# A new list of visits, one kept pair stored earlier, and a re-planned order in a fused attention and expert kernel

## The chip, the cores and the metric

The kernel runs on one core of a Trainium2 chip. The metric is device time in microseconds (us), the median of three runs. Five engines run their own instruction streams in order: PE (TensorE, matmuls; PEld is its weight load), ACT (ScalarE), DVE (VectorE), POOL (GpSimd, idle here but for 0.7 us) and SP (SyncE, which issues every DMA). Streams meet only at semaphores, so an instruction that waits holds up everything behind it on its engine.

## The reference

```python
# x (8, 8, 512, 64), state (8, 8, 32, 64); w_a, w_b (512, 1536), w_out (1536, 512)
scores  = x @ state^T / 8;   a  = softmax over the 32 states;   xread = a  @ state
scores2 = state @ x^T / 8;   a2 = softmax over the 512 tokens;  sread = a2 @ x
t = concat(xread, sread) as (8 * 544 tokens, 512)
out = ((t @ w_a) * (t @ w_b)) @ w_out
```

## The kernel before

**Work.** Everything is done in pairs of reduced-precision parts: a value is split into a high part (`_h`) and the rest (`_l`), and each product is three matmuls (high by high, high by low, low by high). For a batch of 512 tokens `xread` is never formed. Its attention matrix `a` is kept transposed in `at_h`, `at_l` (128 x 2 x 512), and the first layer multiplies it with `state @ w_a` and `state @ w_b`, the "pieces" `p_h`, `p_l`. The 1536 hidden columns are cut in 6 chunks of 256. One batch with one chunk is a *chunk-visit*: 24 wide matmuls `ab<-at,p` and 24 `acc<-wo,g`, 48 in all. The sums over chunks of one visit stay in PSUM (`acc`).

**Chunks.** For chunks 0 and 1 and batches 0 to 3, pieces are made directly (`direct`, L1077) from the batch's states and whole weights. For all else a chunk is "stacked" (L1323): its weights are loaded into `raw`, split into `wq`, and projected (`ms<-wq,sd`) for four batches at once; ACT copies the result out of PSUM to `sw_st`, SP stores it to a scratch `scr` in HBM, and `p_raw` is loaded from there. The output weights of a chunk are two tiles `wo<ft>`, each converted by ACT and DVE (`conv_o`, L1048).

**Visits.** `VISITS` (L33) lists which batch goes through which chunks, in order; `SU` is the extra pass for the 8 x 32 `sread` tokens. A batch that comes back for more chunks has its sums stored (`part<-stg`, in `close`, L1116) at the end of a visit, loaded again (`stg<-part`, `fetch`, L1111) and added. `BEFORE` (L60) names what is recorded ahead of a visit: `attend` makes `a` of a batch, `read` makes its `sread`, `stack` projects a chunk.

**Batch 0's pair.** The buffer `at_h`/`at_l` exists three times, and four batches are open early. So batch 0's pair lives in the tiles `wo6` and `wo10`, which chunk 3 and chunk 5 need later for output weights. `STORE` (L50) says after which visit the pair is written to HBM (`a_dram`); it is read back into `at_h`/`at_l` at batch 0's next visit (`load_a`, L865). Once it is stored, `wo10` also serves as a third buffer beside the two of `sw_st` for projections (L827, L829), until chunk 5 opens.

**Order.** The program first records all calls, then `plan` (L497) orders them: a list scheduler with costs per instruction, one queue per engine and due times that run back from a paced PE. `SHIFTS` (L311) moves due times of numbered groups of instructions and `RELEASES` (L479) holds groups back; both are tables of numbers. When a result of another engine is used, the plan adds `WAKE` = 150 ns (L303, L584, L639). The engines then run their streams in exactly that order, and all recorded calls are issued from one line, so every row of the profile says L1387 (and the same line is L1380 in the changed kernel). In the first microseconds PE runs 80 matmuls `ab<-wo` whose result is not used.

Of the kernel before, what the change touches and what calls it, by code (L numbers as in the profile page):

```python
# [28 lines left out]
SU = B  # L29
# [3 lines left out]
VISITS = [  # L33
    (0, [0]), (1, [0]), (2, [0]), (3, [0, 1]), (2, [1]), (1, [1]), (0, [1, 2]), (1, [2, 3]), (2, [2, 3, 4]),
    (3, [2, 3, 4, 5]), (1, [4, 5]), (2, [5]), (0, [3, 4, 5]),
    (4, [0, 1, 2, 3, 4, 5]), (5, [0, 1, 2, 3, 4, 5]), (6, [0, 1, 2, 3, 4, 5]), (SU, [0, 1]),
    (7, [0, 1, 2, 3, 4, 5]), (SU, [2, 3, 4, 5]),
]
# [11 lines left out]
STORE = {6: (0,)}  # L50
# [9 lines left out]
BEFORE = {  # L60
    9: [("read", 0)], 10: [("read", 1), ("stack", 0)], 11: [("read", 2), ("stack", 1)], 12: [("read", 3), ("attend", 4)],
    13: [("attend", 5)], 14: [("read", 4), ("attend", 6)],
    15: [("read", 5), ("attend", 7), ("read", 6), ("read", 7)],
}
# [230 lines left out]
class Engine:  # L295
# [7 lines left out]
WAKE, SLACK = 150, 1.02  # L303
LOOSE = ("stg",)
# [183 lines left out]
def by_groups(units, table):  # L488
    out, last, n = [], None, -1
    for u in units:  # L490
        n += u.eng == "SP" or u.eng != last
        last = u.eng
        out.append(100.0 * table.get(n, 0))
    return out


def plan(units, pools, t0):  # L497
# [932 lines left out]
```

## Time and profile before

| | before |
|---|---|
| median of 3 runs | 686.49 us (684.2 to 687.44) |
| profiled execution, its own time | 686.96 us |
| its span, first to last instruction | 685.2 us |
| PE / PEld busy | 669.2 us (98%) / 536.3 us (78%) |
| DVE / ACT busy | 471.7 us (69%) / 396.9 us (58%) |
| DMA | 139.62 MB, mean 204 GB/s; `part` 18 stores and 18 loads of 512 KB |
| granted PE clock | 1.00 but for 143.2 to 146.6 us |

Busy is the time in which an engine had an instruction in work. Matmuls are pipelined: one of 128x512 takes 0.39 us from start to its modelled end, but the next starts 0.23 us later, so a busy PE can still be slower than its pace. The pace is read from starts.

### The profile page before, as it was taken

How to read it: one execution, taken by the hardware profiler on the slowest of the kernel's cores; microseconds unless marked ns; L12 is line 12 of the kernel's file. 1: busy time of each engine (PE TensorE's matmuls, PEld its weight loads, DVE VectorE, ACT ScalarE, POOL GpSimd, SP SyncE). 2: the span in 40 equal slices, each digit the busy share in tenths (PEclk: the TensorE clock that was granted, in tenths of full speed). 3: DMA queues.
4: the chain of work that ended last, by engine and by line, in shares of the span. 5: the costliest groups of instructions: out<-in, count | busy, mean ns of one | idle time of the engine just before them, and what ended most of it. 6: DMA issues, size and time to landing. Idle time of an engine off the chain costs nothing.

```text
span 685.2 us, 10452 instructions
## 1 busy us (share of the span) xinstructions
PE 669.2 (98%) x3775; PEld 536.3 (78%) x3775; DVE 471.7 (69%) x922; ACT 396.9 (58%) x743; POOL 0.7 (0%) x6
## 2 busy tenths in 40 slices
PE   7899999989999999999999999999999999999997
PEld 6467678868787777877888778888888889888996
DVE  4999998698866767679989395838343239642682
ACT  4777689598975878746564354635343237532451
POOL 0000000000000000000000000000000000000000
PEclk9999999999999999999999999999999999999999
DMA  7867667989999699868966563531122128210230
GB/s 276 305 218 261 202 201 264 362 319 315 377 343 352 211 351 337 280 195 299 387 219 224 202 205 111 183 130 63 61 70 85 32 92 271 99 31 1 76 110 31
DMA packets 64339, 139.62 MB, mean 204 GB/s; under 512 B 6176, under 2 KB 14624, under 8 KB 64288
## 3 DMA queue, kind: packets, MB, share of 16 engines
q1 hardware_dynamic: 64288, 138.96, 59.3%
q8 instruction: 29, 0.48, 0.3%
q14 instruction: 22, 0.18, 0.1%
HBM read 92.27 MB, written 46.66 MB: 203 GB/s over the span
## 4 chain that ended last, share of the span: by engine, by line
PE 87%; ACT 5%; DMA 4%; DVE 2%; issue 1%; SPq 0%; DVEq 0%; ACTq 0%
PE ab L1387 41%; PE acc L1387 38%; PE ms L1387 8%; DMA x<-xt 2%; DMA raw<-wl 2%; ACT wq L1387 1%; DVE t L1387 1%; ACT g_h L1387 1%; ACT sw_st L1387 1%; ACT p_h L1387 0%; ACT a_sb L1387 0%; ACT t L1387 0%; ACT wo L1387 0%; SPq L1387 0%; ACT stg L1387 0%
## 5 line engine op out<-in xcount | busy, mean ns | idle before, releaser
L1387 PE MATMUL acc<-wo,g_h 128*128 128x512 f32 x818 | 242.5, 391 | 1.5 <-ACT g_h L1387 1.5
L1387 PEld LDWEIGHTS acc<-wo,g_h 128*128 128x128 f32 x818 | 152.5, 188 | 37.2 <-issue 3.3
L1387 PE MATMUL acc<-wo,g_l 128*128 128x512 f32 x409 | 143.8, 390 | 0.0
L1387 PE MATMUL ab<-at_h,p_h 128*128 128x512 f32 x360 | 138.6, 395 | 1.0 <-ACT a_sb L1387 0.9
L1387 PE MATMUL ab<-at_l,p_h 128*128 128x512 f32 x360 | 139.3, 391 | 0.0
L1387 PE MATMUL ab<-at_h,p_l 128*128 128x512 f32 x360 | 135.8, 392 | 0.0
L1387 DVE TENSOR_TENSOR a_sb<-ab,a_sb 128x512 f32<-128x512 f32 (+1 forms) x108 | 71.1, 658 | 76.8 <-PE ab L1387 58.5
L1387 ACT CAST g_h<-a_sb 128x512 fp32r<-128x512 f32 (+1 forms) x108 | 64.2, 599 | 78.4 <-PE acc L1387 61.7
L1387 ACT COPY a_sb<-ab 128x512 f32<-128x512 f32 (+1 forms) x108 | 61.1, 566 | 81.6 <-PE ab L1387 75.1
L1387 DVE TENSOR_TENSOR g_l<-a_sb,g_h 128x512 fp32r<-128x512 f32 (+1 forms) x108 | 70.4, 655 | 53.2 <-PE acc L1387 31.8
L1387 PEld LDWEIGHTS acc<-wo,g_l 128*128 128x128 f32 x409 | 76.8, 188 | 16.3 <-DVE g_l L1387 0.5
L1387 PEld LDWEIGHTS ab<-at_h,p_h 128*128 128x128 f32 x360 | 67.5, 188 | 21.3 <-ACT a_sb L1387 2.8
L1387 PEld LDWEIGHTS ab<-at_h,p_l 128*128 128x128 f32 x360 | 67.8, 189 | 16.4 <-issue 2.1
L1387 PEld LDWEIGHTS ab<-at_l,p_h 128*128 128x128 f32 x360 | 67.9, 189 | 13.9 <-DVE at_l L1387 0.2
L1387 DVE TENSOR_SCALAR t<-t 128x512 int32<-128x512 int32 x128 | 53.0, 421 | 19.7 <-ACT t L1387 17.9
L1387 ACT CAST p_h<-p_raw 128x512 fp32r<-128x512 f32 x80 | 46.6, 620 | 31.3 <-PE ab L1387 27.3
L1387 DVE TENSOR_TENSOR p_l<-p_raw,p_h 128x512 fp32r<-128x512 f32 x80 | 52.4, 684 | 16.4 <-ACT p_h L1387 11.3
L1387 ACT COPY sw_st<-ms 128x512 f32<-128x512 f32 x70 | 39.6, 589 | 11.2 <-PE ms L1387 10.4
L1387 ACT CAST wq<-t 64x512 fp32r<-64x512 f32 (+1 forms) x64 | 39.0, 619 | 9.2 <-DVE t L1387 3.9
L1387 PE MATMUL ms<-wq,sd_h 128*128 128x512 f32 x80 | 32.0, 400 | 3.5 <-ACT wq L1387 2.4
L1387 DVE TENSOR_TENSOR stg<-acc,stg 128x512 f32<-128x512 f32 (+1 forms) x39 | 25.6, 670 | 12.8 <-PE acc L1387 12.7
L1387 ACT ACTIVATE t<-raw 128x512 f32<-128x512 f32 x40 | 26.7, 676 | 9.8 <-DMA raw<-wl 7.0
(99 smaller groups left out, 646.5 us busy)
## 6 DMA issues: line engine op xcount, KB each, us to landing
p_raw<-scr SPq DMA_DIRECT2D x40, 512.0 KB, 4.3
scr<-sw_st SPq DMA_DIRECT2D x70, 256.0 KB, 5.3
raw<-wl SPq DMA_DIRECT2D x32, 512.0 KB, 6.0
part<-stg SPq DMA_DIRECT2D x18, 512.0 KB, 5.3
stg<-part SPq DMA_DIRECT2D x18, 512.0 KB, 6.5
x<-xt SPq DMA_DIRECT2D x15, 576.0 KB, 6.3
out<-stg SPq DMA_DIRECT2D x33, 256.0 KB, 3.0
x<-xn SPq DMA_DIRECT2D x16, 512.0 KB, 6.2
```

Source lines behind the costliest of these rows:

```text
L1387: getattr(obj, method)(*map(real, args), **{k: real(x) for k, x in kw.items()})
```

## The change

The work on the engines is nearly the same: as many PE instructions of each shape, four fewer DVE additions of sums, and 16 instead of 18 `part` stores and as many loads. Of PE's first-layer matmuls, 24 read batch 0's pair as `at` and no longer as `wo`. Of ACT's projection copies 16 and not 10 go to `wo10`. What changes is the order:

- In the new list batch 1 does chunks 0 and 1 in one visit, then batch 0 does chunk 1, then batches 2 and 3 do 0 and 1 together. Chunk 1 is so opened for the third chunk-visit instead of the fifth; batch 2 is attended for the fifth instead of the third, batch 3 for the seventh instead of the fourth. Chunk 2 is first used in the ninth as before, chunk 3 in the twelfth instead of the eleventh, chunk 5 in the seventeenth instead of the eighteenth.
- Batch 0's pair is stored after its second chunk-visit (visit 2) instead of after its third (visit 6), and batch 0 does chunks 2 to 5 at its end instead of 3 to 5.
- `plan` adds `AHEAD` = 350 ns to `WAKE` for an instruction of PE that waits for another engine, from 100 us on.
- The plan's costs of the first loads of `x` change (sooner landing for the first half, 2400 and not 1300 ns of service for the next), and both tables of numbers are new.

```diff
-VISITS = [
-    (0, [0]), (1, [0]), (2, [0]), (3, [0, 1]), (2, [1]), (1, [1]), (0, [1, 2]), (1, [2, 3]), (2, [2, 3, 4]),
-    (3, [2, 3, 4, 5]), (1, [4, 5]), (2, [5]), (0, [3, 4, 5]),
-    (4, [0, 1, 2, 3, 4, 5]), (5, [0, 1, 2, 3, 4, 5]), (6, [0, 1, 2, 3, 4, 5]), (SU, [0, 1]),
-    (7, [0, 1, 2, 3, 4, 5]), (SU, [2, 3, 4, 5]),
-]
+VISITS = [(0,[0]),(1,[0,1]),(0,[1]),(2,[0,1]),(3,[0,1,2]),(2,[2]),(1,[2,3]),(2,[3,4]),(3,[3,4,5]),(1,[4,5]),(2,[5]),(0,[2,3,4,5]),(4,[0,1,2,3,4,5]),(5,[0,1,2,3,4,5]),(6,[0,1,2,3,4,5]),(SU,[0,1]),(7,[0,1,2,3,4,5]),(SU,[2,3,4,5])]
-STORE = {6: (0,)}
+STORE = {2:(0,)}
-    9: [("read", 0)], 10: [("read", 1), ("stack", 0)], 11: [("read", 2), ("stack", 1)], 12: [("read", 3), ("attend", 4)],
...
+BEFORE = {8:[("read",0)],9:[("read",1),("stack",0)],10:[("read",2),("stack",1)],11:[("read",3),("attend",4)],12:[("attend",5)],13:[("read",4),("attend",6)],14:[("read",5),("attend",7),("read",6),("read",7)]}
+AHEAD = 350.0
 SHIFTS = {
-    0: -171837, 1: -10706, 2: -7641, 3: -30373, 5: -2493, 6: 312, 7: -13199, 8: -7514, 9: -4002, 10: -5829, 11:
...
 RELEASES = {
-    14: 124, 37: 91, 38: 112, 45: 123, 67: 14, 147: 581, 173: 438, 183: 2, 193: 710, 204: 735, 216: 341, 300:
+    1: 7, 6: 108, 37: 122, 38: 106, 43: 55, 50: 68, 54: 295, 61: 11, 62: 154, 63: 231, 72: 319, 92: 346, 152:
...
+def wake(u, t):
+    return WAKE + (AHEAD if u.eng == "PE" and t > 100e3 else 0.0)
...
-            t = max(t, free_at[k - 1] + WAKE)
+            t = max(t, free_at[k - 1] + wake(units[i], free_at[k - 1]))
...
-                        late(nc.sync.dma_start(out=x[:, g, h], in_=xt[self.b, g, :, h]), 740 if h == 0 else 0)
+                        u = nc.sync.dma_start(out=x[:, g, h], in_=xt[self.b, g, :, h])
+                        u.land -= 900
+                        late(u, 740 if h == 0 else 0)
...
-                    u.serve += 1300 if self.b == 0 else 0
+                    u.serve += 2400 if self.b == 0 else 0
```

**First place: ACT ahead of the first projections of chunk 3, before.** `wo6_1576` is an output weight of chunk 3 that goes into the tile of batch 0's pair; `wq_1615` and `wq_1628` are chunk 3's split weights, `sw_st` the copies of projections.

```order
L1387 COPY sw_st_1553<-ms_1547 128x512
L1387 CAST wo6_1576<-t2_1311 128x512
L1387 COPY sw_st_1583<-ms_1573 128x512
L1387 ACTIVATE t1_1592<-raw_1296 128x512
L1387 ACTIVATE t1_1599<-raw_1316 128x512
L1387 COPY sw_st_1583<-ms_1578 128x512
L1387 CAST wq_1615<-t2_1602 64x512
L1387 ACTIVATE a_tr_1621,m2_1587<-e2_1518,m2_1587 128x4x4x32
L1387 CAST wq_1628<-t2_1612 64x512
```

PE at the same place. `ab_1562` is the last tile of batch 0's first layer that reads `wo6`; `ms_1656` is the first projection of `wq_1615`.

```order
L1387 MATMUL ab_1562<-wo6_235,p_l_1512 128x512
L1387 MATMUL ms_1573<-wq_1213,sd_h1_816 128x512
L1387 MATMUL ms_1573<-wq_1213,sd_l1_1111 128x512
L1387 MATMUL ms_1578<-wq_1213,sd_h1_816 128x512
L1387 MATMUL ms_1578<-wq_1213,sd_l1_1111 128x512
L1387 MATMUL acc_1585<-wo2_956,g_h_1356 128x512 x2
```

ACT now, where the same output weight is `wo6_1343`.

```order
L1380 ACTIVATE t1_1333<-wo9_1240 128x512
L1380 CAST wo6_1343<-t2_1329 128x512
L1380 COPY a_sb_1350<-ab_1210 128x512
L1380 COPY sw_st_1298<-ms_1340 128x512
L1380 CAST wo7_1359<-t2_1347 128x512
L1380 COPY stg_1368<-acc_1125 128x512
L1380 COPY stg_1373<-acc_1235 128x512
L1380 COPY wo10_1378<-ms_1370 128x512
L1380 ACTIVATE t1_1384<-raw_1314 128x512
```

Before, the cast waits for the last `ab_1562` that reads `wo6`, in batch 0's chunk 2, the ninth chunk-visit; 22 wide matmuls lie between that one and `ms_1656`. Now the last PE row that reads the pair, `ab_866<-wo6_209`, stands some 180 rows of PE's order ahead of this cast, in batch 0's chunk 1.

**Second place: ACT in the first chunk-visits, before.** `wo11<-x` copies a batch's states out of its loaded `x`; `x_417` is batch 3's. `g_h_492` is the second hidden tile of batch 0.

```order
L1387 COPY a_sb_470<-ab_432 128x512
L1387 CAST at_h_482<-a_tr_472 128x512
L1387 COPY wo11_124<-x_417 64x2x32 x2
L1387 CAST g_h_492<-a_sb_470 128x512
L1387 COPY wo11_124<-x_417 64x2x32 x2
```

The same place now; `x_507` is batch 3's, and `raw_402` is a weight of chunk 1.

```order
L1380 COPY a_sb_496<-ab_437 128x512
L1380 ACTIVATE t1_501<-raw_402 128x512
L1380 COPY e2_510<-ms_480 128x512
L1380 CAST at_h_439<-a_tr_518 128x512
L1380 CAST g_h_535<-a_sb_496 128x512
L1380 COPY wo11_116<-x_507 64x2x32 x2
```

The copy from a batch's `x` stood between the product and its high part and now stands behind it; a read of a loaded weight stands there instead.

**Third place: PE where a later batch's scores begin (`ms<-x`), before.**

```order
L1387 MATMUL acc_3430<-wo8_1771,g_l_3254 128x512
L1387 MATMUL ab_3441<-at_h_615,p_h_3198 128x512
L1387 MATMUL ab_3443<-at_h_615,p_h_3198 128x512
L1387 MATMUL ab_3441<-at_l_629,p_h_3198 128x512
L1387 MATMUL ab_3441<-at_h_615,p_l_3205 128x512
L1387 MATMUL ab_3441<-at_h_615,p_h_3198 128x512
L1387 MATMUL ab_3441<-at_l_629,p_h_3198 128x512
L1387 MATMUL ms_3451<-x_3388 32x512
L1387 MATMUL ms_3453<-x_3388 32x512
```

PE now, at the scores of batch 5: `ms_3540` and `ms_3555` are projections in the two `ms` buffers that `ms_3573` and `ms_3575` take over.

```order
L1380 MATMUL ms_3540<-wq_3252,sd_h1_775 128x512
L1380 MATMUL ms_3540<-wq_3252,sd_l1_793 128x512
L1380 MATMUL ab_3529<-at_l_810,p_h_3153 128x512
L1380 MATMUL ab_3529<-at_h_787,p_l_3170 128x512
L1380 MATMUL ms_3555<-wq_3252,sd_h1_775 128x512
L1380 MATMUL ms_3555<-wq_3252,sd_l1_793 128x512
L1380 MATMUL ms_3573<-x_3445 32x512
L1380 MATMUL ms_3575<-x_3445 32x512
```

ACT now, between the copies that free those two buffers.

```order
L1380 COPY sw_st_3549<-ms_3540 128x512
L1380 CAST p_h_3553<-p_raw_3189 128x512 x2
L1380 COPY sw_st_3549<-ms_3555 128x512
L1380 CAST g_h_3568<-a_sb_3518 128x512
L1380 COPY a_sb_3635<-ab_3616 128x512
```

Before, no projection stands close ahead of the scores; now two do, with two casts between their copies on ACT.

## Rows read from the trace of the kernel before

**Rows 1.** The page, part 1: busy us (share of span), instructions.

```profile
PE 669.2 (98%) x3775; PEld 536.3 (78%) x3775; DVE 471.7 (69%) x922; ACT 396.9 (58%) x743; POOL 0.7 (0%) x6
```

**Rows 2.** Stretches: length; PE, PEld, DVE, ACT, POOL busy (count); clock, DMA share, GB/s.

```profile
45.00:139.00 94.00, 93.53 (x514) 70.00 (x513) 82.68 (x165) 73.11 (x135) 0.00 (x0) 1.00 0.74 251
139.00:147.00 8.00, 5.61 (x18) 4.17 (x17) 7.53 (x15) 7.74 (x14) 0.00 (x0) 0.79 1.01 375
147.00:270.00 123.00, 120.98 (x640) 96.36 (x639) 91.11 (x181) 95.87 (x177) 0.00 (x0) 1.00 0.92 322
270.00:684.00 414.00, 411.48 (x2345) 340.56 (x2343) 256.88 (x495) 192.16 (x360) 0.00 (x0) 1.00 0.44 147
```

**Rows 3.** Timeline of PE, 138 to 147 us: start, length, instruction [idle before <-releaser].

```profile
138.51 0.62 PE L1387 MATMUL acc<-wo,g_l 128*128 128x512 f32 x2
138.97 0.62 PE L1387 MATMUL acc<-wo,g_h 128*128 128x512 f32 x2
139.42 0.39 PE L1387 MATMUL acc<-wo,g_l 128*128 128x512 f32 x1
142.20 0.50 PE L1387 MATMUL ms<-wq,sd_h 128*128 128x512 f32 x1 [2.39 <-ACT wq L1387]
...
143.26 0.63 PE L1387 MATMUL ab<-at_h,p_h 128*128 128x512 f32 x1
...
146.64 0.40 PE L1387 MATMUL ab<-at_h,p_l 128*128 128x512 f32 x1
```

**Rows 4.** Timeline of ACT, 134 to 142 us.

```profile
134.86 0.62 ACT L1387 CAST wo<-t 128x512 fp32r<-128x512 f32 x1 [2.10 <-PE ab L1387]
...
141.53 0.62 ACT L1387 CAST wq<-t 64x512 fp32r<-64x512 f32 x1
```

**Rows 5.** Timeline of ACT and PE, 38 to 40 us.

```profile
38.72 0.50 ACT L1387 COPY wo<-x 64x64 f32<-64x64 f32 x2 [1.38 <-DMA x<-xt]
...
39.24 0.62 ACT L1387 CAST g_h<-a_sb 128x512 fp32r<-128x512 f32 x1
...
39.91 0.50 PE L1387 MATMUL acc<-wo,g_h 128*128 128x512 f32 x1 [1.10 <-ACT g_h L1387]
```

**Rows 6.** Timeline of PE: its longer waits between 147 and 270 us.

```profile
178.65 0.50 PE L1387 MATMUL ab<-at_h,p_h 128*128 128x512 f32 x1 [0.25 <-ACT a_sb L1387]
...
207.18 1.19 PE L1387 MATMUL acc<-wo,g_h 128*128 128x512 f32 x4 [0.37 <-ACT g_h L1387]
...
251.42 0.50 PE L1387 MATMUL ms<-wq,sd_h 128*128 128x512 f32 x1 [0.97 <-ACT sw_st L1387]
```

**Rows 7.** Groups of instructions: count | busy us, mean ns of one | idle before.

```profile
L1387 DVE TENSOR_TENSOR stg<-acc,stg 128x512 f32<-128x512 f32 x37 | 24.9, 683 | 11.4 <-PE acc L1387 11.3
L1387 DVE SCALAR_TENSOR_TENSOR t<-raw,t 128x512 f32<-128x512 uint32 x40 | 27.3, 684 | 0.4
L1387 DVE TENSOR_SCALAR t<-t 128x512 int32<-128x512 int32 x128 | 53.0, 421 | 19.7 <-ACT t L1387 17.9 <-ACT wq L1387 0.2
L1387 ACT COPY sw_st<-ms 128x512 f32<-128x512 f32 x70 | 39.6, 589 | 11.2 <-PE ms L1387 10.4 <-ACT y L1387 0.4
L1387 ACT CAST p_h<-p_raw 128x512 fp32r<-128x512 f32 x80 | 46.6, 620 | 31.3 <-PE ab L1387 27.3 <-DMA p_raw<-scr 3.5
```

**Rows 8.** DMA issues: count, KB each, median us from issue to landing.

```profile
part<-stg SPq DMA_DIRECT2D x18, 512.0 KB, 5.3
stg<-part SPq DMA_DIRECT2D x18, 512.0 KB, 6.5
at_l<-a_dram SPq DMA_DIRECT2D x1, 512.0 KB, 5.0
```

**Rows 9.** Stretches in which DVE is fullest, as in the second group.

```profile
40.00:100.00 60.00, 59.52 (x383) 41.75 (x391) 57.51 (x109) 47.64 (x85) 0.00 (x0) 1.00 0.64 211
100.00:127.00 27.00, 27.00 (x132) 21.74 (x117) 19.50 (x44) 21.84 (x44) 0.00 (x0) 1.00 0.79 268
40.00:127.00 87.00, 86.53 (x507) 63.49 (x508) 77.01 (x152) 69.48 (x129) 0.00 (x0) 1.00 0.69 229
```

More of the change, by code (lines that the diff above doesn't have):

```diff
@@ L58 @@
 SPLIT = (0, 1)
-BEFORE = {
-    9: [("read", 0)], 10: [("read", 1), ("stack", 0)], 11: [("read", 2), ("stack", 1)], 12: [("read", 3), ("attend", 4)],
-    13: [("attend", 5)], 14: [("read", 4), ("attend", 6)],
-    15: [("read", 5), ("attend", 7), ("read", 6), ("read", 7)],
-}
+BEFORE = {8:[("read",0)],9:[("read",1),("stack",0)],10:[("read",2),("stack",1)],11:[("read",3),("attend",4)],12:[("attend",5)],13:[("read",4),("attend",6)],14:[("read",5),("attend",7),("read",6),("read",7)]}
 _cells = {}
@@ L638, in plan @@
         for j, w in suc[i].items():
-            r = t if not w else done[i] + WAKE if units[j].eng != e or e == "SP" else t + u.occ if e == "PE" else done[i]
+            r = t if not w else done[i] + wake(units[j], done[i]) if units[j].eng != e or e == "SP" else t + u.occ if e == "PE" else done[i]
             ready[j] = max(ready[j], r)
```

331 rows, old and new, of tables (RELEASES, SHIFTS) are left out of this document.

## The prediction

> **What bounds the kernel now.** I read the page's busy times first. PE is busy for 669.2 of 685.2 us, DVE for 471.7, ACT for 396.9 [rows 1]. So PE sets the end, and only what PE waits for, or runs slowly in, can be won; work that the change moves on other engines counts only through PE.
>
> Next I cut the span into stretches [rows 2]. From 270 us to 684 PE is busy for 411.48 of 414.00, with DMA at 0.44: little is to be had there. In the other stretches PE idles less than the sums suggest, since its ends are modelled; I took its losses from the starts of its matmuls. Two wide ones take 0.46 us from start to start (138.51, 138.97, 139.42 in [rows 3]), 0.23 each.
>
> The largest loss lies at 139.42. The next matmul starts at 142.20, 2.78 us later instead of 0.23, having waited for ACT's `wq`: 2.55 us lost. The granted clock of 139 to 147 us is 0.79 [rows 2], the only stretch of the four below 1.00, and the matmuls show where: from 143.26 to 146.64 eight start in 3.38 us instead of 1.82, so the clock is at 1.2 and not 2.4 GHz there, right behind the wait. That loses 1.56 us more. The place costs 4.1 us in all. What made `wq` late stands on ACT: the cast into `wo6` began at 134.86 after idling 2.10 us for PE's `ab`, and ACT reached the `wq` that PE waited for at 141.53 [rows 4]. The cast waited because batch 0's pair lay in that tile and PE was still reading it.
>
> The second place is at 39.91: PE waits 1.10 us for `g_h`, which ACT did at 39.24, behind the copy of `x` at 38.72 that had waited 1.38 us for its load [rows 5]. After it come three waits of 0.25, 0.37 and 0.97 us [rows 6]. DVE is nearly as full as PE in one stretch: 57.51 of 60 us from 40 to 100, then 19.50 of 27 [rows 9].
>
> **The change part by part.** *Batch 0's pair stored sooner.* In the first order piece the cast into `wo6` waited on a PE row 22 wide matmuls ahead of the first projection of chunk 3. Now PE's last reading row lies some 180 rows ahead of the cast, so it waits only for DVE's `t2`. The 2.10 us idle of ACT goes, hence PE's 2.55 us, and with it the 1.56 us at the low level, which follow only a wait here. What is late next there is the chain of splits on DVE, which I treat below. Gain: 4.1 us.
>
> *The copy from `x` behind `g_h`.* In the second order piece a read of a weight stands where the copy stood, and the copy behind `g_h`. The 1.10 us go if that weight has landed. Gain 1.1, bounds 0 to 1.1.
>
> *The margin.* `AHEAD` plans PE's dependent instructions 350 ns later, so that a wait up to that length is filled with other matmuls: 0.25, 0.35 of 0.37, 0.35 of 0.97. Gain 0.9, bounds 0 to 1.6 (all three waits gone).
>
> *New: scores behind projections.* In the third order piece, ACT must copy `ms_3540`, cast `p_h` twice and copy `ms_3555` before `ms_3575` can start. By [rows 7] that is 0.589 + 2 x 0.620 + 0.589 = 2.42 us after the end of the last `ms_3540` matmul, which comes 0.16 us later than the next start (0.39 us long, a pace of 0.23). PE has five matmuls to do from that start, 1.15 us. The wait is 2.42 + 0.16 - 1.15 = 1.4 us; behind it on PE stand the scores and all later matmuls, since its stream is in order. Bounds 0 (if the two casts were late and no wait showed) to 1.4 plus a fall of the clock as in [rows 3], 3.0. I take 1.4.
>
> *New: a long run on ACT.* Where batch 2 or 3 has its sums copied out early on, ACT now has fourteen instructions in a row before an `a_sb` that PE's next product needs, some 14 x 0.55 = 7.7 us by durations like those of [rows 7], against 6.2 us of PE's work. Bounds 0 to 1.4, the lower if ACT arrives early; I take 0.5.
>
> *Reloading the pair.* It is needed again at batch 0's last visit: its load can be issued some 31 wide matmuls, 7.0 us, ahead of its use, and the load landed in 5.0 us [rows 8]. Cost 0; if the issue stands in line on SP or DMA is full, up to 1.5.
>
> *Fewer sums.* Four DVE adds less, 4 x 0.683 = 2.7 us [rows 7]; two stores and loads less, 2.1 of 139.62 MB, 5.3 and 6.5 us from issue to landing [rows 8]. PE waits for none of these in the rows, so I take nothing; were DVE or DMA the bound there, it would be 2.7 us.
>
> *Chunk 1 and chunk 3 sooner, chunk 5 sooner.* The splits of their weights move forward on DVE. The eighth chunk-visit begins at 127 us before. By then DVE must now have done its 221st instruction instead of its 207th: 14 more (4 at 0.684, 6 at 0.421 [rows 7], four small ones), 8.0 us, of which 3.0 us were already done by that time. So 5.0 us more must fit into 40 to 127, where DVE idled 87.00 - 77.01 = 10.0 us [rows 9]. It fits, so the cost is 0; if DVE can't use those gaps, the price is the second rival's.
>
> DVE and PE can be weighed in another way. In 40 to 100 us DVE is busy for 57.51 of 60, PEld for 41.75, PE for 59.52 [rows 9]. The Trainium skill (Perfetto Trace Analysis, Identifying the Most-Contended Engine) says that the engine of highest occupancy is the one to improve first, and that for TensorE weight loads are to be judged and not matmul busy time. By that rule DVE at 96% binds that stretch and not PE at 70%, and 5.0 us more of its work would cost about that much. The trace is against it so far: PE stands idle for 0.48 of those 60 us, so DVE, however full, kept up.
>
> *Sum.* - 4.1 - 1.1 - 0.9 + 1.4 + 0.5 = - 4.2 us. The profiled execution took 686.96 us, 0.5 above the median; 686.96 becomes 682.8, and the median of 686.49 becomes **682.3 us**.
>
> **Rivals.** *Better than forecast.* The two new waits don't show, as ACT idles for much of the time (396.9 of 685 busy): 682.3 - 1.9 = 680.4. Against it: both are worked from durations, not from shares.
>
> *The gain is given back.* The order is new everywhere, and each wait of 1 to 2 us brings the low clock behind it. With 1.4 at the scores, 1.4 at the run on ACT, 1.5 at the reload and one fall of the clock, 1.6, the loss is 5.9 of the 6.1 gained: 686.3, no change. For it: before, one 2.39 us wait did bring a fall [rows 3]; against it: the waits of 1.10 and 0.97 [rows 5, 6] brought none, at a clock of 1.00 in their stretches [rows 2, 9].
>
> *DVE becomes the bound, and it is slower.* The mechanism is that DVE can't fill its gaps, because its splits wait for loads and for ACT's halves. From 40 us on 77.0 + 5.0 = 82.0 us of DVE work must be done before the eighth chunk-visit; 57.5 are done by 100, and if its share after that stays at 19.50 / 27.00 = 72%, the other 24.5 take 34 us. The visit starts at 134 instead of 127, 7.0 late, and a wait of that kind brings the fall of the clock, 1.6. That gives 682.3 + 8.6 = 690.9. It decides from 4.2 us of lateness on; below that the kernel is still not slower. For it: DVE's 96% just before. Against it: after 100 us it is not full, so the work that was ahead of need can be moved.
>
> **How the numbers follow.** The forecast gets 0.50, with its own range of 679.5 to 685; better 0.17; the gain given back 0.18; DVE as the bound 0.15. Half a per cent, about what a measurement of this kernel can tell from no change, is 3.4 us: faster ends at 683.1, slower begins at 689.9. Of the forecast's range about a third lies above 683.1. So faster is 0.17 + 0.33 = 0.50, the same 0.17 + 0.18 = 0.35, slower 0.15. The range of 8 in 10 goes from 677.5 (both new waits absent and the 2.7 us of the dropped adds won as well) to 689.8, where most of the last rival lies outside.
>
> **What would show it right or wrong.** Around the first projections of chunk 3, PE without a wait of over 1 us and the granted clock at 1.00: the first term is right. PE without the 1.10 us in the first 45 us: the second. A wait of about 1.4 us on `ms<-x` by ACT's `sw_st`, in the fifth batch's last chunks before its successor: the third place. At batch 0's last visit, a wait on the load of `at_l` would show the reload short. For the last rival, PE would wait several us for DVE's `t` or ACT's `wq` between 100 and 150 us, with DVE near 96% to the end of that stretch. The forecast is wrong if the total of PE's waits ahead of 270 us isn't about 4 us less than before, or if that total goes and the span doesn't.

## The result and the profile after

The changed kernel takes 690.41 us, the median of 18 runs (687.53 to 693.67), against 687.11 for the kernel before in 18 runs. The ratio is 1.0051, 95% interval 1.0036 to 1.0066. It is slower by half a per cent, where the prediction said faster by 0.6%. The profiled execution took 691.42 us with a span of 689.6, against 685.2 before; the medians differ by 3.3 us, the two profiles by 4.4, so about 1 us of what follows is the choice of the execution. Nine of the eighteen runs had a mean granted clock of 0.990 to 0.993 and took 691.5 us on average, the other nine 0.994 or 0.995 and 688.8; the profiled one, at 0.992, belongs to the first nine.

The page's busy times after answer to [rows 1]:

```profile
PE 671.3 (97%) x3775; PEld 536.0 (78%) x3775; DVE 470.1 (68%) x918; ACT 394.9 (57%) x743; POOL 0.7 (0%) x6
```

DVE has four instructions less and every other count is the same, so the loss is one of order. The stretches answer to [rows 2], with the last one cut finer:

```profile
45.00:139.00 94.00, 91.50 (x504) 67.83 (x502) 87.08 (x176) 77.44 (x143) 0.00 (x0) 1.00 0.68 238
139.00:147.00 8.00, 7.57 (x33) 5.67 (x32) 7.86 (x17) 7.01 (x14) 0.00 (x0) 1.00 0.88 272
147.00:270.00 123.00, 122.55 (x713) 99.47 (x712) 86.07 (x166) 95.01 (x178) 0.00 (x0) 1.00 0.96 335
284.00:312.00 28.00, 26.56 (x183) 19.12 (x181) 21.31 (x48) 18.56 (x37) 0.00 (x0) 1.00 0.95 326
312.00:325.00 13.00, 10.17 (x43) 6.33 (x43) 8.48 (x17) 3.24 (x6) 0.00 (x0) 0.87 1.01 370
325.00:684.00 359.00, 359.00 (x1975) 299.67 (x1974) 213.15 (x407) 154.82 (x291) 0.00 (x0) 1.00 0.34 112
```

The kernel before in two of these, as a measure:

```profile
284.00:312.00 28.00, 28.00 (x193) 21.53 (x192) 21.82 (x43) 15.18 (x28) 0.00 (x0) 1.00 0.65 219
312.00:325.00 13.00, 13.00 (x71) 10.12 (x69) 12.68 (x25) 9.35 (x19) 0.00 (x0) 1.00 0.95 333
```

From 139 to 270 us PE is better off than before (0.88 us idle where it was 4.41), and then it stands for 4.3 us between 284 and 325, where before it never stood. The DMA share of 284 to 312 is 0.95 instead of 0.65.

To compare two orders I took every matmul's start, counted the work before it at the pace (0.227 us for a wide one, the short ones at their usual start to start), and called the difference the time lost. The two programs have the same work on PE, so the losses can be set side by side by work done:

| PE's work done, us | lost before | lost after | difference |
|---|---|---|---|
| 0 to 50 | 14.4 | 14.1 | -0.3 |
| 50 to 110 | 0.4 | 2.2 | +1.8 |
| 110 to 150 | 4.3 | 2.5 | -1.8 |
| 150 to 260 | 5.6 | 2.2 | -3.4 |
| 260 to 300 | 0.1 | 8.6 | **+8.5** |
| 300 to the end | 1.1 | 0.9 | -0.2 |

Up to 260 us of work the changed kernel is 3.7 us ahead. That this is near the 4.2 forecast is partly luck: all terms but the +1.4 at the scores lie in this part, and they come to -5.6. It then loses 8.5 us in 40 us of work. PE's timeline there:

```profile
284.84 0.27 PE L1380 MATMUL ms<-ident,y 128*128 128x128 f32 x1
286.55 0.50 PE L1380 MATMUL acc<-wo,g_h 128*128 128x512 f32 x1 [1.44 <-ACT g_h L1380]
...
316.38 0.39 PE L1380 MATMUL acc<-wo,g_l 128*128 128x512 f32 x1
318.99 0.73 PE L1380 MATMUL ab<-at_h,p_h 128*128 128x512 f32 x2 [2.22 <-DMA at_h<-a_dram]
320.27 0.50 PE L1380 MATMUL ab<-at_l,p_h 128*128 128x512 f32 x1 [0.54 <-DMA at_l<-a_dram]
...
320.96 0.63 PE L1380 MATMUL ab<-at_h,p_h 128*128 128x512 f32 x1
321.39 0.63 PE L1380 MATMUL ab<-at_l,p_h 128*128 128x512 f32 x1
```

Two places make 6.3 of the 8.5 us. At 318.99 and 320.27 PE waits for the reload of batch 0's pair, 2.38 and 0.71 us over its pace, and then starts a matmul every 0.43 us instead of 0.23, at the lower clock (0.87 in the stretch), 1.6 us more: 4.7 us. At 286.55 it waits for `g_h`, 1.6 us over its pace. Of the rest, 1.1 us are the scores at 311.35 (below). For the wait at 286.55 ACT shows why:

```profile
282.92 0.66 ACT L1380 ACTIVATE t<-raw 128x512 f32<-128x512 f32 x1 [1.42 <-DMA raw<-wl]
283.48 1.13 ACT L1380 CAST p_h<-p_raw 128x512 fp32r<-128x512 f32 x2
...
285.87 0.62 ACT L1380 CAST g_h<-a_sb 128x512 fp32r<-128x512 f32 x1
```

ACT stood 1.42 us for a weight that landed 6.6 us after its issue at 276.32, with `g_h` five instructions behind. For the pair, here is SP, after and then before:

```profile
305.65 0.34 SPq L1380 DMA_DIRECT2D out<-stg  x1
308.32 0.32 SPq L1380 DMA_DIRECT2D stg<-part  x1
...
310.52 1.04 SPq L1380 DMA_DIRECT2D turned<-s_p  x1
311.60 1.13 SPq L1380 DMA_DIRECT2D at_h<-a_dram  x1
312.77 0.45 SPq L1380 DMA_DIRECT2D at_l<-a_dram  x1
```

```profile
318.84 0.59 SPq L1387 DMA_DIRECT2D at_h<-a_dram  x1
...
320.10 0.59 SPq L1387 DMA_DIRECT2D at_l<-a_dram  x1
```

Batch 0's last visit has four chunks now and begins one chunk sooner, so its reload goes out 7.2 us sooner. SP stood on the way to it. Of its waits between 305 and 312 us (in total, times, longest) this one is ahead of `stg<-part` at 308.32, for a store that was issued at 300.65 and took 7.6 us to land:

```profile
SPq L1380 <- DMA out<-stg: 2.2, 1, 2.2
```

Four issues follow, and then the reload at 311.60. In the program SP's issues of `turned` and `at_h` also wait for the DMA eight places ahead to land. Those are the two halves of `x`, which took 8.4 and 9.1 us, but they had landed at 309.6 and 311.0, before SP came to the two issues at 310.52 and 311.60, so they did not hold it up. PE would have started on `at_h` one pace behind 316.38, at 316.61, which is 5.0 us after the issue. The reload lands in 7.3 and 7.4 us, not in the 5.0 of [rows 8], and 7.3 us where PE left 5.0 is about the 2.38 us that it lost. The kernel before had little to spare here either: its `at_h` landed in 4.4 us, at 323.2, and PE's first use is this one:

```profile
323.57 0.61 PE L1387 MATMUL ab<-at_h,p_h 128*128 128x512 f32 x2
```

What DMA is issued from 270 to 316 us, before and after (count, KB each, us to landing):

```profile
x<-xt SPq DMA_DIRECT2D x4, 576.0 KB, 7.0
scr<-sw_st SPq DMA_DIRECT2D x7, 256.0 KB, 4.9
out<-stg SPq DMA_DIRECT2D x5, 256.0 KB, 6.3
```

```profile
scr<-sw_st SPq DMA_DIRECT2D x15, 256.0 KB, 5.9
x<-xt SPq DMA_DIRECT2D x4, 576.0 KB, 7.8
out<-stg SPq DMA_DIRECT2D x8, 256.0 KB, 6.2
sd_h<-wl SPq DMA_DIRECT2D x2, 512.0 KB, 7.4
sd_l<-wl SPq DMA_DIRECT2D x1, 512.0 KB, 7.5
at_h<-a_dram SPq DMA_DIRECT2D x1, 512.0 KB, 7.3
at_l<-a_dram SPq DMA_DIRECT2D x1, 512.0 KB, 7.4
```

With the groups not shown here the issues come to 11.1 and 15.0 thousand KB. What the DMA engines moved in these 46 us is 11.75 MB before and 14.88 MB after. The new order has 15 stores of projections in this stretch for 7, three weight loads and the reload that were later before.

### The profile page after: what moved, and what is told of

It is laid out like the page before. It is cut to its first block, busy times and chain, and to the rows that moved or that the text cites. A ratio compares the mean times of both kernels' runs of the same rounds, so it can differ in the third digit from the quotient of the medians.

```text
span 689.6 us, 10408 instructions
## 1 busy us (share of the span) xinstructions
PE 671.3 (97%) x3775; PEld 536.0 (78%) x3775; DVE 470.1 (68%) x918; ACT 394.9 (57%) x743; POOL 0.7 (0%) x6
## 4 chain that ended last, share of the span: by engine, by line
PE 81%; DVE 7%; DMA 6%; ACT 5%; issue 1%; SPq 1%; DVEq 0%; ACTq 0%
PE ab L1380 39%; PE acc L1380 36%; PE ms L1380 6%; DMA raw<-wl 4%; DVE t L1380 2%; ACT wq L1380 2%; DVE m L1380 1%; DMA at_l<-a_dram 1%; DVE s_p L1380 1%; DVE wq L1380 1%; ACT t L1380 1%; SPq L1380 1%; ACT sw_st L1380 0%; DMA raw<-w_out 0%; ACT p_h L1380 0%
## 5 line engine op out<-in xcount | busy, mean ns | idle before, releaser
L1380 PE MATMUL acc<-wo,g_h 128*128 128x512 f32 x818 | 254.2, 391 | 1.4 <-ACT g_h L1380 1.4
L1380 PE MATMUL acc<-wo,g_l 128*128 128x512 f32 (+1 forms) x409 | 151.6, 390 | 0.1
L1380 PE MATMUL ab<-at_h,p_h 128*128 128x512 f32 x368 | 142.4, 396 | 4.4 <-DMA at_h<-a_dram 2.2
L1380 PE MATMUL ab<-at_l,p_h 128*128 128x512 f32 x368 | 142.6, 392 | 0.5 <-DMA at_l<-a_dram 0.5
L1380 PE MATMUL ab<-at_h,p_l 128*128 128x512 f32 x368 | 141.0, 392 | 0.0
L1380 PEld LDWEIGHTS ab<-at_h,p_h 128*128 128x128 f32 x368 | 69.2, 188 | 25.3 <-ACT a_sb L1380 4.8
L1380 PEld LDWEIGHTS ab<-at_h,p_l 128*128 128x128 f32 x368 | 69.5, 189 | 15.6 <-issue 0.8
L1380 PEld LDWEIGHTS ab<-at_l,p_h 128*128 128x128 f32 x368 | 69.5, 189 | 15.1 <-DMA at_l<-a_dram 1.0
L1380 ACT COPY sw_st<-ms 128x512 f32<-128x512 f32 x64 | 36.8, 586 | 10.0 <-PE ms L1380 8.6
L1380 PE MATMUL ms<-wq,sd_l 128*128 128x512 f32 x80 | 31.2, 390 | 0.0
```

The costliest lines, as they stand in the source:

```text
L1380: getattr(obj, method)(*map(real, args), **{k: real(x) for k, x in kw.items()})
```

## The experiments

Each edits the finished order or the data of one of the two kernels. Ratios are to the kernel before; the changed kernel stands at 1.0051 (1.0036 to 1.0066), and where the interval of an edited changed kernel overlaps this one, the gain is not clear of the noise. The diffs are shortened. Edits of order are written as (engine, row, new row) or as (engine, first row, rows in their new order), counted on that engine: a few lines behind the planner apply them to each engine's list, and all dependencies are kept.

**1. The reload sooner on SP.** Was the pair only badly placed?

```diff
+MOVES = (('SP', 257, 253), ('SP', 258, 254))  # at_h, at_l: from row, to row
```

> The changed kernel with one edit: in SP's finished order the two loads of batch 0's pair stand four places earlier, ahead of a scratch store, an output store, a scratch store and a store of turned; nothing else moves. Theory A (the reload stood in line on SP: its buffer was free at about 308.7 us, but it was issued at 311.6, behind two issues that had to wait for the loads of x issued eight places before): it is now issued at about 308.7, lands at about 316 even with its 7.3 us, PE's waits of 2.22 and 0.54 us and the 1.6 us at the low clock behind them go, 690.4 becomes 686.0. Theory B (the DMA engines are full there, and anything issued sooner lands as much later, or pushes another load past its use): 1 us or less is won, 689.5 or more.

688.85 us, ratio 1.0027 (1.0006 to 1.0049): 1.6 us less, which is not clear of the noise. `at_h` is in time, `at_l` is not:

```profile
318.23 0.61 PE L1401 MATMUL ab<-at_h,p_h 128*128 128x512 f32 x2
320.67 0.50 PE L1401 MATMUL ab<-at_l,p_h 128*128 128x512 f32 x1 [1.82 <-DMA at_l<-a_dram]
```

Its issue, 0.48 us behind `at_h`, landed 9.6 us later. The clock did not fall here, which is most of what this place won in the trace. The whole traced execution, 691.23 us, is the slowest of the twelve: at 26 us PE waited 4.66 us where the changed kernel waited 3.01. The edit left `stg<-part` and SP's wait for the store ahead of the pair, so `at_h` went out at 310.54 and not at 308.7. In this trace order on SP is a part, and the transfer itself is the other.

**2. Less to transfer, same order.** Eight output stores write 32 of their 512 columns, and the rest of these rows is left out.

```diff
+if sp and k in (221, 228, 235, 237, 246, 247, 251, 254):  # SP rows, out<-stg
+    kw = {a: x[:, :32] for a, x in kw.items()}
```

> The changed kernel, with eight output stores between 267 and 310 us (by the trace) writing 32 of their 512 columns, so the rest of these rows is left out of the output; about 2.0 MB less in that stretch, some 6 us of DMA time by its rate of 0.34 MB per us. The order of every engine is unchanged. Theory B (DMA full): the weight load that ACT waited for until 282.9 lands over 1 us sooner and the reload is issued and lands sooner, both of PE's losses there (1.6 and 4.7 us) mostly go: 684 to 686. Theory A (order on SP alone): the loads of x land a little sooner, so the issue moves by under 1 us; 688 to 690.

686.23 us, ratio 0.9991 (0.9971 to 1.0012): 4.2 us less than the changed kernel. The reload's waits shrink and the clock stays up:

```profile
316.39 0.73 PE L1385 MATMUL ab<-at_h,p_h 128*128 128x512 f32 x2 [0.65 <-DMA at_h<-a_dram]
317.47 0.50 PE L1385 MATMUL ab<-at_l,p_h 128*128 128x512 f32 x1 [0.35 <-DMA at_l<-a_dram]
```

The reload was issued 2.2 us sooner with no row of SP moved:

```profile
305.42 0.34 SPq L1385 DMA_DIRECT2D stg<-part  x1
...
309.36 0.45 SPq L1385 DMA_DIRECT2D at_h<-a_dram  x1
```

The store that SP had stood 2.2 us for, one of the eight, now landed in time, so `stg<-part` went out 2.9 us sooner. The pair itself landed in 7.0 and 7.6 us, hardly faster or slower than in the changed kernel: what was won here came by the sooner issue. The wait of 1.43 us at 286 us stayed. Of the eight stores only two stand ahead of that weight, so that half of the expectation was not put to the test.

**3. `g_h` ahead of the late weight.**

```diff
+MOVES = (('ACT', 405, 400), ('DVE', 450, 445))  # g_h, g_l
```

> The changed kernel with one edit: at 282.9 us (by the trace) ACT's g_h stands ahead of the read of a weight that has not landed instead of five places behind it, and DVE's g_l likewise five places sooner. If PE's 1.44 us wait there is only that g_h stands behind a late load on an in-order engine, it goes and the time falls by 0.6 to 1.6 us (the wq cast behind it comes 0.6 us later and may be waited for instead): 688.8 to 689.8. If the late load is needed at once by PE through its own split, the wait only changes its name: 690.4.

691.37 us, ratio 1.0054 (1.0025 to 1.0083): nothing won. The edit was put too far ahead, since `g_h`'s buffer was still being read by PE:

```profile
283.52 0.62 ACT L1401 CAST g_h<-a_sb 128x512 fp32r<-128x512 f32 x1 [2.04 <-PE acc L1401]
284.05 0.67 ACT L1401 ACTIVATE t<-raw 128x512 f32<-128x512 f32 x1
```

ACT stood 2.04 us for PE instead of 1.42 for the weight, and PE waited 2.29 us for `sw_st` in place of 1.44 for `g_h`.

**4. Four places at once.**

```diff
+MOVES = (('SP', 257, 253), ('SP', 258, 254), ('ACT', 405, 400), ('DVE', 450, 445),
+         ('ACT', 121, 119), ('ACT', 164, 162))  # the last: a_sb, a projection's copy
```

> The changed kernel with the edits of the two others (reload four places up on SP, g_h five places up on ACT and g_l on DVE) and two more on ACT: at 91 us the copy a_sb that PE waited 1.24 us for stands two places sooner, at 119.8 us the copy that empties a projection buffer (0.82 us) two places sooner. If these four places are what the change lost, 690.4 - 4.4 - 1.1 - 1.0 - 0.7 = 683.2, below the kernel before. If waits move on to the next late instruction, 686 to 688.

689.64 us, ratio 1.0045 (1.0025 to 1.0065). In the trace `a_sb` at 91 us won 0.8 us; the projection's copy moved its wait of 0.82 us on to the next copy (0.68); the `g_h` edit lost again, with a fall of the clock behind it.

**5. SP cleared for the reload, all work done.**

```diff
+MOVES = (('SP', 246, [248, 249, 250, 253, 257, 258, 255, 256, 246, 247, 251, 259, 254, 260, 261, 262, 252]),)
```

> The changed kernel with SP's finished order edited in one stretch: the pair's two reloads stand ahead of the scratch store, and five output stores and one load of sums that nothing near needs (1.75 MB, some 5 us of DMA at 0.34 MB per us) stand behind them, the loads of x in front keep their places. All the work is done, only its order on SP differs. Theory B in its second form (the reload is late by the queue and by the full DMA together; order alone won 1.8 us of its place, and leaving 2 MB out won 3.7): the waits of 2.22 and 0.54 us and the 1.6 at the low clock go down to under 0.5 us together, the time falls by about 4.5 us to 686. Rival (the x and weight loads in the same stretch are what fills it, output stores are only passed on): a wait of 1 to 2 us stays on the reload and the deferred stores delay another load; 688 to 689.

688.56 us, ratio 1.0023 (1.0006 to 1.0040). The edit defers four output stores and the load of sums, 1.5 MB, not the five and 1.75 MB of the expectation. In the trace the reload is in time, the loss from 290 to 300 us of work is 1.0 us for 4.9, and the span is 685.6, as expected:

```profile
307.33 0.58 SPq L1402 DMA_DIRECT2D at_h<-a_dram  x1
```

The pair still took 6.6 and 7.4 us to land, so order alone was enough for this wait. The median won 1.9 us, not 4.5, which is not clear of the noise; the traced execution lies 1.2 us below its median, that of the changed kernel 1.0 above its own.

**6. The same, with `g_h` right behind the late weight.**

```diff
+MOVES += (('ACT', 400, [400, 405, 404, 401, 402, 403]), ('DVE', 445, [445, 450, 446, 447, 448, 449]),
+          ('ACT', 119, [121, 119, 120]))
```

> As the run with SP's order edited, and two places on ACT and DVE: at 283 us g_h and the copy of a projection stand right behind the read of the late weight, ahead of two casts p_h and one wq (g_l on DVE likewise), and at 91 us the copy a_sb stands two places sooner. If the losses are independent: 686 - 1.5 - 0.8 = 683.7, below the kernel before by 0.4%. If the late weight is needed by PE at once, the 1.5 stay: 685.

687.58 us, ratio 1.0013 (0.9999 to 1.0026). This is 2.8 us less than the changed kernel, clear of the noise, with every byte moved. At 285 to 288 us PE now waits 1.06 and 0.52 us, and a new place has come, at a weight load that stands behind the deferred stores:

```profile
321.02 0.66 ACT L1402 ACTIVATE t<-sd_h 128x512 f32<-128x512 f32 x1 [2.27 <-DMA sd_h<-wl]
321.59 0.65 ACT L1402 ACTIVATE t<-sd_l 128x512 f32<-128x512 f32 x1
322.14 0.61 ACT L1402 CAST g_h<-a_sb 128x512 fp32r<-128x512 f32 x1
```

PE waited 1.71 us for that `g_h`. In experiment 5, with the same order on SP, it waited 0.43 us there, so that the deferred stores alone make this wait is not shown.

**7 and 8. The margin without its tables.**

```diff
-AHEAD = 350.0
+AHEAD = 0.0          # 7, in the changed kernel
+AHEAD = 350.0        # 8, with wake() in the kernel before
```

> The changed kernel planned with the margin at 0 instead of 350 ns, all else (visits, both tables) as in it. The prediction's price of the margin is 0.9 us, so 691.3; by the traces PE lost 4.3 us less between 140 and 280 us than before, and if the margin made that, 694. The tables of shifts were made with the margin, so a new order can cost more on its own: any loss is an upper bound of what the margin gives.

> The kernel before, planned with the margin of 350 ns from 100 us on and its own tables. If the margin alone fills short waits: 0.9 to 2 us faster, 685. If tables made for another plan no longer fit: slower by some us, with new waits at new places.

711.09 us (ratio 1.0356, 1.0331 to 1.0380) and 708.27 us (1.0314, 1.0290 to 1.0337). Either change costs over 20 us, in a few stalls: in the first 10 us between 110 and 120 us of work, in the second 12 between 150 and 160. The second also waits 5.8 and 1.9 us for the pair's reload at 342 to 345 us. The tables fit one plan only, and these runs do not price the margin.

**9. The kernel before with the missing bytes.** This tests the cause from the other side, though not the bytes alone, as the twelve copies also stand in line on SP.

```diff
+if k in (231, 232, 233, 234, 235, 237, 238, 240, 242, 244, 247, 249):  # SP rows
+    x = dram.pool.tile([P, 512], I32, name=f"more{k}", bufs=1)
+    base.sync.dma_start(out=x, in_=w_out[:P, :256].bitcast(I32))
```

> The kernel before, with twelve copies of 256 KB of the output weights into unused scratch in HBM added on SP between 281 and 317 us (by its trace), 3.1 MB or some 9 us of DMA, about what the changed kernel moves more than it between 270 and 316 us (15.0 against 11.1 MB by the issues). Nothing else reads or waits for them; the order of PE, ACT and DVE is the same. Theory B (that the DMA engines are full there is what makes loads late): PE gets waits of 1 to 4 us on loads between 290 and 330 us, the pair's reload or a weight, and perhaps a fall of the clock: 689 to 692. Rival (the order of SP and of ACT in the changed kernel makes the loss, not the bytes): under 1 us, 687 to 688.

691.58 us, ratio 1.0076 (1.0059 to 1.0093): 5.2 us slower, with no instruction of PE, ACT or DVE moved. The same wait appears at the same load:

```profile
325.32 0.84 PE L1388 MATMUL ab<-at_h,p_h 128*128 128x512 f32 x2 [2.50 <-DMA at_h<-a_dram]
```

```profile
284.00:312.00 28.00, 28.00 (x191) 21.29 (x190) 21.95 (x44) 15.17 (x28) 0.00 (x0) 1.00 0.83 278
...
325.00:360.00 35.00, 34.62 (x155) 26.37 (x156) 28.40 (x61) 17.59 (x32) 0.00 (x0) 0.95 0.81 289
```

The DMA share of 284 to 312 us went from 0.65 to 0.83, and the clock fell behind the wait (0.95 in the later stretch). `at_h` was issued at 319.56, 0.7 us later than before, and landed in 5.7 us for 4.4, so the line on SP and the transfer both grew.

**10. All moves, stores behind the weight loads.**

```diff
+MOVES = (('SP', 246, [248, 249, 250, 253, 257, 258, 255, 256, 246, 259, 260, 261, 262, 247, 251, 254, 252]),
+         ('ACT', 400, [400, 405, 404, 401, 402, 407, 403, 406, 409, 408]), ('ACT', 437, [437, 438, 441, 439, 440]),
+         ('ACT', 119, [121, 119, 120]), ('DVE', 445, [445, 450, 446, 447, 448, 449]), ('DVE', 510, [514, 510, 511, 512, 513]))
```

> The changed kernel with moves of rows alone: the reload ahead of stores on SP, output stores and a load of sums behind two weight loads; on ACT g_h ahead of the reads of two late weights at 321 us and two g_h and an a_sb sooner at 283 to 287 us, a_sb two places sooner at 91 us, DVE's g_l to match. If each wait was an in-order engine standing at a late load, 687.6 - 1.7 - 1.5 = 684.4, below the kernel before. If the bytes set the pace, another load is late in its place: 686.5 to 688.

690.52 us, ratio 1.0061 (1.0041 to 1.0081). Up to 310 us of work this order is 2.5 us ahead of the kernel before. Then `turned` is the late one, DVE stands 4.30 us for it, and PE waits for DVE:

```profile
334.10 0.72 DVE L1402 STREAM_TRANSPOSE s_p<-ms 128x512 f32<-128x512 f32 x1 [4.30 <-DMA turned<-s_p]
```

```profile
338.44 2.08 PE L1402 MATMUL acc<-wo,g_l 128*128 128x512 f32 x4 [2.26 <-DVE g_l L1402]
```

**11 and 12. Both kernels without their tables.**

```diff
-SHIFTS = {0: ..., ...}
-RELEASES = {1: ..., ...}
+SHIFTS = {}
+RELEASES = {}
```

> The changed kernel with both tables of numbers (shifts and releases) empty: visits, storing, margin and costs as in it, the order by the planner's rules alone. To be compared with the same of the kernel before. Both are expected some 15 to 40 us slower than their tuned orders. If the list of visits by itself brings the fuller DMA ahead of batch 0's last visit, the DMA share of the 40 us before the pair's reload is higher here than in the other; if the tables brought it, it is alike.

> The kernel before with both tables of numbers empty, the other half of that comparison. If the new list is worth anything without its tables, this one is slower than the other by some us.

731.82 and 747.92 us, one run each, so without an interval. By the planner's rules alone the changed kernel, with its margin and costs, is 16 us the faster. The DMA share of the 40 us ahead of the reload is 0.85 and 0.81, nearly alike, where with the tables it is 0.96 and 0.73. This points to the tables and not to the list of visits by itself, but on one trace each it does not show it. Here too PE waits for the pair, 2.0 and 5.1 us.

**13 and 14. The first two terms in the kernel before.**

```diff
+MOVES = (('ACT', 48, [50, 48, 49]),)                                       # 13
+MOVES += (('ACT', 190, [190, 191, 193, 194, 192]), ('DVE', 224, [225, 226, 224]), ('DVE', 236, [237, 236]))  # 14
```

> The kernel before with one edit: ACT's g_h at 39 us stands ahead of the two copies from a batch's x that wait for its load, instead of behind them (what the changed kernel does there, and the prediction's second term). If the term stands alone: PE's 1.10 us wait at 39.9 us goes and the time falls by about 1.1 us, 685.8 against 686.9. If it is passed on: the wait at 40 us goes, another of about its size comes before 140 us (the stall there waits for weights and not for PE), and the time is 686.9.

> As that run, and at 140 us ACT's two wq casts stand one place ahead of the second g_h, DVE's last split one place ahead of g_l, and a reduction ahead of the output weight's low part that waits for PE. PE's wait of 2.39 us for wq should shrink by 0.6 us; the fall of the clock behind it stays. 685.2 if the gains add up; 686.3 or more if the first is passed on.

686.80 us (ratio 1.0001, 0.9985 to 1.0018) and 685.98 us (0.9996, 0.9978 to 1.0014). Both are the same as before within the measurement. In the trace of 13 the wait at 40 us is gone, and it stays gone: at 120 us of work the loss is 13.3 us for 14.8. A gain of 1.1 us is too near the interval's half width, also 1.1 us, to be seen in the times. In 14 PE's wait for `wq` is 1.88 us for 2.39. All of that place could not be undone by moving rows: the cast into `wo6` can't be put behind later reads of weights, as these reuse its buffers.

## Why the prediction was wrong

The step that failed is the reload of the pair: "Cost 0; if the issue stands in line on SP or DMA is full, up to 1.5." It cost 4.7 us in the trace. Both conditions held at once, and the price left out the fall of the clock behind the wait (1.6). Of the 7.0 us by which the issue was to be ahead of the use, 5.0 were left, as SP stood 2.2 us for a store; and the landing took 7.3 us and not 5.0. The landing time of 5.0 us came from the kernel before, where the load went out 7 us later; nowhere did I ask how full DMA would be at the new place. I had cut the profile at 270 us and set the rest aside as a stretch with DMA at 0.44. That average hid 0.57 to 1.03 up to 340 us. The sign that the prediction named for this, a wait on the load of `at_l`, came, and so did its last way of being wrong: PE lost about 4 us less ahead of 270 us, and the span did not follow.

That the late reload is the main loss is shown from both sides: 2 MB less gives back 4.2 us (experiment 2), moves of rows on SP, ACT and DVE 2.8 us (6), and twelve more copies cost the kernel before 5.2 us at the same load (9). How much of the lateness is SP's line and how much the slower landing is not shown: experiments 2 and 5 bring the load forward by a sooner issue alone, 9 changes both, and none changes the landing alone. That a fuller DMA makes the landing slow is argued from the shares, and these do not give it alone: while the load was on its way the share was 0.95 in experiment 2 and 1.03 in experiment 9, and it took 7.0 and 5.7 us.

From the forecast's -4.2 to the +4.4 us between the two profiles are 8.6 us. The reload is 4.7 of them and the weight at 283 us 1.6, for which the prediction had no term. Ahead of 260 us of work 1.9 less was won than the terms say, and the scores cost 0.3 less than priced. That makes 7.9.

Point by point:

- **First place, -4.1.** The mechanism held: no wait for `wq` behind the pair, and the clock of 139 to 147 us is 1.00. The size was off. The loss from 110 to 150 us of work fell by 1.8 us, since four waits of 0.10 to 0.33 us stand there now. A further one of 0.82 us, for a copy of a projection behind a late weight, comes just ahead, at 120 us.
- **`g_h` and the copy from `x`, -1.1.** The 1.10 us wait went, also in the trace of experiment 13, whose times don't show it. The changed kernel has a new wait of 3.01 us for DVE's `s_p` at 23.93 us, and a fall of the clock of its own in 17 to 35 us (0.81), for which there was no term, so its first 50 us gained only 0.3.
- **The margin, -0.9.** From 150 to 260 us of work 3.4 us were won. How much of it is the margin stays open.
- **Scores behind projections, +1.4.** The mechanism held, and 1.1 us of the 1.4 came: the sixteen matmuls took 2.20 us from 311.35 for 1.09 us before, and the third of them waited for ACT's second copy, which ended at 312.41:

```profile
311.35 2.20 PE L1380 MATMUL ms<-x 64*32 64x512 f32 x16
```

- **The run on ACT, +0.5.** 1.4 us over the pace, the upper bound (its 7.7 less 6.2 is 1.5):

```profile
91.77 0.50 PE L1380 MATMUL ab<-at_h,p_h 128*128 128x512 f32 x1 [1.24 <-ACT a_sb L1380]
```

- **DVE** did not become the bound: between 100 and 150 us PE waits for ACT alone. Its 8.0 us of moved work are not borne out by the rows named, where four at 0.684 and six at 0.421 make 5.3 us. The last rival's 690.9 was near the time by another mechanism. The nearest by mechanism was the gain given back, with the reload and a fall of the clock in it, but with 1.5 us for the reload and nothing for the weight at 283 us (1.6).
- **Fewer sums** gained nothing that shows: the 2.1 MB less over the whole kernel stand against 3.1 MB more between 270 and 316 us.

What stays open: how SP's line and the slower landing share the lateness, what makes the landing slow, and whether any order of these visits is faster than the kernel before. None of the fourteen runs was faster by more than the measurement's interval.

## What to carry to other kernels

Price a load that is moved at its new time and not by its landing time at the old one: ask what the issuing engine waits for just ahead of it, and how full DMA is, with the DMA share cut into stretches as fine as the loads that it delays. Where DMA is full, moving rows can make another load the late one: three orders in turn had the pair, `sd_h` and `turned` late, though one of them won back 2.8 of 3.3 us. An order that rests on such tables is fitted together as a whole: one constant changed without its tables cost over 20 us.

## What the runs showed of the hardware

The same wait does not always bring the lower clock. In experiment 13 PE waited 2.40 us for the same `wq` as in [rows 3], and the clock stayed at 1.00:

```profile
140.69 0.50 PE L1409 MATMUL ms<-wq,sd_h 128*128 128x512 f32 x1 [2.40 <-ACT wq L1409]
```

```profile
136.00:146.00 10.00, 7.26 (x31) 5.26 (x30) 9.51 (x20) 9.69 (x18) 0.00 (x0) 1.00 0.99 364
```

So the 1.56 us that the prediction put to that place are there in some executions only. This does not explain why the runs of the kernel before spread over 5 us: of the 87 beside the experiments, the thirty with the lowest granted clock took 686.6 us on average, the thirty with the highest 686.5.

The two loads of the pair, 512 KB each, landed in 4.4 and 5.0 us in the kernel before and in 7.3 and 7.4 in the changed one, where the DMA share was 1.01; in experiment 1 the second took 9.6. SP issues in order, so a slow transfer also delays others: the changed kernel's reload stood behind a load of sums for which SP waited 2.2 us, until a 256 KB store had landed. By the program an issue also waits for the DMA eight places ahead, and in experiment 9 SP stood 0.8 us for a half of `x` in this way.
